# A hand-written order of 942 steps, laid anew: step order, engines, PSUM banks and output transfers of a fused attention and gMLP kernel

## The chip, the cores and the metric

The kernel runs on one core of a Trainium2 chip. The metric is device time in microseconds (us) of one execution; the times shown are the median, lowest and highest of several. A core has five engines that run their own instruction streams and meet at semaphores: TensorE (PE, with its weight loads shown apart as PEld), VectorE (DVE), ScalarE (ACT), GpSimd (POOL) and SyncE (SP), which here issues most DMA transfers.

## The reference

Input x is 2048 x 448 in bf16, with H = 16 heads of Dh = 28, and Fh = 896 channels in each half of the gMLP.

```python
mod = silu(c) @ w_mod                       # six rows: sa, ca, ga, sb, cb, gb
h = layernorm(x) * (1 + ca) + sa
q, k, v = heads(h @ wqkv)
phi(t) = concat(softmax(t @ w_phi), softmax(-(t @ w_phi)))       # for each head
kv = phi(k)^T @ v ;  z = sum over s of phi(k)
o = (phi(q) @ kv) / (phi(q) . z + 1e-6)
x = x + ga * (o @ wo)
h = layernorm(x) * (1 + cb) + sb
y = gelu(h @ w_in) ;  z1, z2 = y[:, :896], layernorm(y[:, 896:])
g = w_sp @ z2 + b_sp                        # w_sp is 2048 x 2048: mixes positions
out = x + gb * ((z1 * g) @ w_out)
```

## The kernel before, in words

**An order written out by hand.** The whole fast path is one string, ORDER (from line 482). Each word is a step: a name, its arguments after a colon, the engine after a slash (V is DVE, S is ACT, G is POOL, Y is the DMA queue of SP) and, after an @, the PSUM bank that a product goes to. A loop at the end (lines 1282 to 1294) takes the words one by one and calls the function of that name, with scheduling by hand: each engine executes its own words in the order in which they stand. There is no planner. A word's place therefore sets what it is queued behind on its engine; what it waits for on other engines follows from the tiles and banks that it reads and overwrites. PSUM has eight banks: @0 to @7 name one, @A0, @A1, @A2 and @C the pairs 0-1, 2-3, 4-5 and 6-7. A product that goes to a bank waits until the reader of that bank's former content is done.

Positions are worked in 16 tiles of 128 (index i), or in 8 pairs (index p). The stages, in order, with the step names that the prediction uses:

- *K stage.* l1s, l1e, l1r, l1a: statistics and application of the first layer norm. T1 (line 890): DMA transpose of tiles to hT, on SP. kM (908) is k times its weights, kE and kF (911) the two exponentials on ACT, kS (922, DVE), kR (926, DVE) and kP (929, DVE or POOL) the softmax. vM (916) and vC (919) make v. kA (939) accumulates phi(k)^T v of all tiles in PSUM. csB and ccB (801) make the shift and scale columns of the second norm, esB and ecB (807) read them, bc (855, 857) spreads them; gr (967) and ge (970) make the gate rows ga and gb. wos and wts (973) multiply wo and w_out by them.
- *Attention's output.* KV (945, DVE) masks the accumulated product into the right-hand side of nM. qM (956), qE and qF (961) make phi(q). For each tile nM (984, PE), nX (988, ACT), nC (991, DVE); for each pair nS (995) and nV (1000) on DVE; then for each tile nT (1003, DVE, reads the banks of nM) and nA (1010, DVE or POOL), which writes half a pair of f_oo. T2 (1013) transposes a pair on SP. wN and wM (1025, 1029, PE) multiply it by wo; wR (1034 ACT, 1036 DVE) evicts to x and sums, wQ (1041 ACT, 1043 DVE) sums squares.
- *Second norm and gMLP in.* lA, lB, lC, lD (1049 to 1058) and l2r (1061, POOL) make mean and reciprocal deviation, l2a (1065) applies them, T3 (1069) transposes a pair on SP, hS (815 ACT, 818 DVE) applies the columns. zM (1079) is the z2 half, zG (1082, ACT) its gelu, zQ its squares, zA to zD and zW its statistics, zN (1097, DVE or POOL) the normalization. yM (1104) and yG (1107) are the z1 half. W:t,u (1113) are the 32 transposing loads of w_sp on SP; W:0 has a tile of its own, W:1 and W:3 go to the tile of phi(q) (f_Eq) and W:2 to that of w_in (f_win), so they wait until these are read out.
- *Spatial product.* w_sp @ z2 in two halves of the output positions (p = 0 and 1). Six of the seven column blocks are made by a Strassen-Winograd scheme: tT (1162) are its differences of z2 blocks, sS (1174) its sums of w_sp blocks, pM:p,f,k (1185) its seven products of eight matmuls each, for f = 0 to 2; pc (1205, ACT) copies one out of PSUM, pb (1208 and 1209, POOL) adds the bias, uA, uB, uW and cA (1212, DVE) add products up, cX (1237, DVE or POOL) multiplies by z1. gM (1121) and gG (1127) are the seventh block. guard (1240) to guard3 (1252) compute the flag by which a general path would be taken: guard2 is a product of one number into a bank, guard3 reads it there, `read` (1255) loads it at the end.
- *Output.* oM (1134) is seven matmuls for a tile of 128 positions, oE (1150, DVE) adds x, oD (1153) sends the 112 KB tile out on SP. The last tile is done in two halves, oH, oG (1143, DVE) and oF (1147, on ACT's queue).

What the diff touches in code is only the string; it is read here:

```python
for word in ORDER.split():
    word, _, slot = word.partition("@")
    word, _, en = word.partition("/")
    nm, _, arg = word.partition(":")
    ...
    STEPS[nm](*[int(v) for v in arg.split(",") if v], **kw)
```

Of the kernel before, what the change touches and what calls it, by code (L numbers as in the profile page):

```python
# [490 lines left out]
kA:1@A1 qE:1 kR:3 vM:6@6 l1e:12,16/V kS:4 vM:7@4 ld:wmgb/Y l1r:12,16 kE:6 kP:3/V kA:2@A1 kS:5 kE:7 vM:4@5 l1a:15/G kF:6 kA:3@A1 l1a:12/G vC:5 kR:4 kR:5
kM:10@1 kF:7 l1a:13/V kP:5/G kS:6 vC:7 T1:12,14 kM:9@0 vC:6 kM:8@4 kP:4/V l1a:14/G vM:8@7 kR:6 kE:8 kS:7 vM:11@6 kF:8 kP:6/G T1:14,16 vC:4 kM:11@4 kR:7 kE:9
kS:8 kA:4@A1 ld:win1/Y kP:7/G kA:5@A1 kE:10 kM:13@5 kR:8 kF:9 kF:10 kS:9 ld:wo/Y vM:9@0 kP:8/G kA:6@A1 kS:10 vC:9 kA:7@A1 vC:8 W:0,2 kM:12@1 kE:11 kR:9
kR:10 kF:11 kM:14@0 kP:9/V kE:12 W:0,1 kP:10/V kA:8@A1 kF:12 kA:9@A1 kS:11 kE:14 kM:15@1 bc:0/S kS:12 vM:10@4 W:0,5 kE:13 kF:14 vM:12@7 kR:11 kF:13 kR:12
# [4 lines left out]
nM:6@A0 wR:1/S nT:5 nA:4/G nM:7@A1 nX:6 nX:7 wR:0/S nC:6 nC:7 wN:1@C nA:5/V T2:2 wQ:0/S nS:3 nV:3 nT:6 wQ:1/S nM:9@A2 wR:3/S nT:7 nM:8@A0 nA:6/G nX:9 nX:8
wR:2/S nC:9 nC:8 wN:2@A1 nA:7/V T2:3 wQ:2/S lA:2,4/G nS:4 lA:0,2/G nV:4 lB:2,4/G lB:0,2/G nT:8 wQ:3/S qM:7@C wR:5/S lC:2,4/G lC:0,2/V bc:1/G nT:9 wR:4/S  # L500
nA:8/V lD:0,2/V lD:2,4/V nM:11@A0 nA:9/V qF:7 l2r:2,4 wQ:5/V nM:10@A1 T2:4 qM:6@A2 l2a:2/V nX:11 l2a:3/G nX:10 qE:7 nC:10 nC:11 lA:4,6/G T3:1 wQ:4/S nS:5
l2r:0,2 nV:5 wN:3@C nT:10 qE:6 l2a:0/G nT:11 l2a:1/G qF:6 lB:4,6/G T3:0 wR:6/S lC:4,6/G nM:12@A0 hS:1/V nM:13@A1 wR:7/S nA:11/V nA:10/V nX:12 zM:1@A2+C
# [839 lines left out]
```

## Time and profile before

| | us |
|---|---|
| time, median of 3 runs (lowest to highest) | 248.39 (248.27 to 248.64) |
| time of the profiled execution | 248.15 |
| its span in the profile | 246.3 |
| busy: PE | 232.2 |
| busy: DVE | 195.8 |
| busy: ACT | 109.0 |
| busy: POOL | 137.3 |

The span runs from the first to the last instruction that the profile holds; the time contains some 2 us around it. A line number such as L1003 is a line of the kernel. In the tables of windows each row is a stretch of the span, its length, the busy time of PE, PEld, DVE, ACT and POOL, the granted TensorE clock, the busy share of the DMA engines and GB/s. A row of waits reads: the engine and line that waits, the engine and line it waits for, us in total, times, longest. A row of a timeline begins with start and duration in us; x8 means that so many instructions of one line stand together in it. In rows of the chain of waits the same two numbers stand ahead. An f_oo<-f_t is a tile written from a tile read.

### The profile page before, as it was taken

The numbers are of one execution on the slowest core, as the hardware profiler recorded it, in microseconds if no ns is written. First come the engines' busy times: TensorE is split into PE (matmuls) and PEld (weight loads), VectorE is DVE, ScalarE is ACT, GpSimd is POOL, SyncE is SP. The second block draws the span as 40 slices with busy tenths as digits, with TensorE's granted clock in tenths as the row PEclk, the third lists the DMA queues.
The fourth block names the chain that finished last, engine by engine and source line by source line (L and its number), as shares of the span: only waits on it lengthen the run. The fifth ranks groups of instructions, "written<-read, shape, count | busy, mean of one in ns | idle before, by whom it ended". The sixth has DMA issues, their size and how long they took to land.

```text
span 246.3 us, 4824 instructions
## 1 busy us (share of the span) xinstructions
PE 232.2 (94%) x1831; PEld 126.6 (51%) x1840; DVE 195.8 (79%) x383; ACT 109.0 (44%) x228; POOL 137.3 (56%) x173
## 2 busy tenths in 40 slices
...
GB/s 173 260 286 129 79 215 187 279 206 251 92 102 76 125 167 109 60 42 163 220 178 115 24 3 1 0 54 116 149 188 44 3 73 39 0 3 1 1 68 94
DMA packets 68130, 26.94 MB, mean 109 GB/s; under 512 B 56385, under 2 KB 67970, under 8 KB 68098
## 3 DMA queue, kind: packets, MB, share of 16 engines
...
## 4 chain that ended last, share of the span: by engine, by line
PE 72%; DVE 13%; DMA 6%; issue 3%; ACT 1%; POOL 1%; SPq 1%; DVEq 0%; POOLq 0%; ACTq 0%
PE f_psum L1185 26%; PE f_psum L1134 8%; PE f_psum L1104 8%; PE f_psum L1079 6%; PE f_psum L1121 6%; PE f_psum L908 4%; PE f_psum L916 4%; DMA f_zone<-in_w_mod_dram 3%; DVE f_t L1003 3%; PE f_psum L956 3%; PE f_psum L939 2%; PE f_psum L1029 2%; DMA f_oo<-f_oo 1%; DMA f_hT<-f_xpad 1%; PE f_psum L831 1%
## 5 line engine op out<-in xcount | busy, mean ns | idle before, releaser
L1185 PEld LDWEIGHTS <-f_zone 128*128 128x128 bf16 x192 | 18.7, 98 | 22.6 <-issue 0.4
L1185 PE MATMUL f_psum<-f_wsp,f_zone 128*128 128x512 bf16 x116 | 27.2, 379 | 0.2
L1185 PE MATMUL f_psum<-f_hT,f_Eq 128*128 128x512 bf16 x95 | 22.3, 379 | 0.1
L1079 PE MATMUL f_psum<-f_win,f_hT 64*128 64x448 bf16 x224 | 22.0, 349 | 0.4 <-DVE f_hT L818 0.4
L1104 PE MATMUL f_psum<-f_hT,f_win 64*128 64x256 bf16 (+1 forms) x294 | 22.1, 305 | 0.1
L1134 PE MATMUL f_psum<-f_wout,f_zone 128*128 128x448 bf16 x105 | 20.7, 352 | 0.0
L1237 POOL TENSOR_TENSOR f_zone<-f_win,f_zone 128x512 bf16<-128x512 f32 x9 | 11.7, 1309 | 15.0 <-DVE f_win L1212 15.0
L1205 ACT COPY f_win<-f_psum 128x512 f32<-128x512 f32 x2 | 1.2, 587 | 42.0 <-POOL f_zone L1237 37.4
L961 ACT ACTIVATE f_Eq<-f_psum 112x1024 bf16<-112x1024 f32 x16 | 16.0, 1026 | 5.8 <-PE f_psum L956 5.8
L911 ACT ACTIVATE f_zone<-f_psum 128x448 bf16<-128x448 f32 x32 | 16.3, 560 | 4.3 <-DVE f_zone L929 2.2
L1104 PEld LDWEIGHTS <-f_win 64*128 64x128 bf16 x294 | 14.4, 94 | 7.3 <-DVE f_hT L818 0.2
L1003 DVE TENSOR_TENSOR f_t<-f_psum,f_w 128x896 bf16<-128x896 f32 x16 | 16.8, 1086 | 0.6
L922 DVE TENSOR_REDUCE f_ksum<-f_zone 128x32 f32<-128x896 bf16 x16 | 16.8, 1067 | 0.5 <-ACT f_zone L911 0.5
L929 POOL TENSOR_TENSOR f_zone<-f_zone 128x896 bf16<-128x896 bf16 x8 | 13.8, 1741 | 5.8 <-DVE f_zone L926 5.5
L1079 PEld LDWEIGHTS <-f_hT 64*128 64x128 bf16 x224 | 11.0, 94 | 10.1 <-DVE f_hT L818 0.5
L1082 ACT ACTIVATE f_zone<-f_psum 128x896 bf16<-128x896 f32 x16 | 14.6, 914 | 3.0 <-PE f_psum L1079 3.0
L1107 ACT ACTIVATE f_zone<-f_psum 128x512 bf16<-128x512 f32 (+1 forms) x21 | 14.3, 739 | 3.0 <-PE f_psum L1104 2.8
L1185 PEld LDWEIGHTS <-f_Eq 128*128 128x128 bf16 x96 | 9.4, 98 | 11.3
L956 PE MATMUL f_psum<-f_hT,f_zone 113*128 113x512 bf16 (+1 forms) x64 | 15.0, 379 | 0.0
L1134 PEld LDWEIGHTS <-f_zone 128*128 128x128 bf16 x105 | 10.2, 98 | 9.3
L908 PE MATMUL f_psum<-f_zone,f_hT 113*128 113x448 bf16 (+1 forms) x64 | 14.0, 352 | 0.2 <-ACT f_zone L911 0.2
L916 PE MATMUL f_psum<-f_zone,f_hT 113*128 113x448 bf16 (+1 forms) x64 | 14.0, 352 | 0.0
...
## 6 DMA issues: line engine op xcount, KB each, us to landing
...
f_wout<-in_B_w_out_dram SPq DMA_DIRECT2D x1, 784.0 KB, 5.4
...
```

Of the source, the lines that this page charges most:

```text
L908: nc.tensor.matmul(t[:, 0, 0:D], lhsT=hT[0:KR[m], i, m, :], rhs=Wk[0:KR[m], m, :], start=(m == 0), stop=(m == KC - 1))
L911: nc.scalar.activation(out=Er[i % NR][:, s, :], in_=ps["k" + str(i)][:, 0, 0:D], func=ACT.Exp, scale=1.0 - 2.0 * s)
L916: nc.tensor.matmul(t[:, 0, 0:D], lhsT=hT[0:KR[m], i, m, :], rhs=wv[0:KR[m], m, :], start=(m == 0), stop=(m == KC - 1))
L922: nc.vector.tensor_reduce(out=ksum[:, i], in_=Er[i % NR][:].rearrange("p s (c f h) -> p (s c) h f", c=4, h=HP), axis=AX.X, op=ALU.add)
L956: nc.tensor.matmul(t[:, u, :], lhsT=Wq[0:KR[m], m, cc * CB:cc * CB + P], rhs=hT[0:KR[m], 4 * st:4 * st + 4, m, :], start=(m == 0), stop=(m ...
L961: nc.scalar.activation(out=Eq[st // 2][0:CB, 2 * c2:2 * c2 + 2, s, (st % 2) * 512:(st % 2 + 1) * 512], in_=ps["q" + str(n)][0:CB, :, :], f ...
L1003: nc.vector.tensor_tensor(out=tr[i % 2][:], in0=numv(i)[:, :, :, 0:DH], in1=wr[i // 2 % 2][:, i % 2].unsqueeze(3).to_broadcast([P, 2, H, D ...
L1079: nc.tensor.matmul(t[u][:, hf, 0:D], lhsT=hP[r, p, blk(j, u), :], rhs=win2[r, j, hf * D:(hf + 1) * D], start=(j == 0), stop=(j == KB - 1))
L1104: nc.tensor.matmul(t[:, u, 0:k * P], lhsT=win1[r, j, fc * P:(fc + 1) * P], rhs=hP[r, p:p + k, blk(j, u), :], start=(j == 0), stop=(j == KB ...
L1121: nc.tensor.matmul(g[:, 0, 0:b - a], lhsT=later["z2n"][:, s_, fc * P:(fc + 1) * P], rhs=wspT[t][:, s_, a:b], start=(s_ == 0), stop=(s_ == ...
L1134: nc.tensor.matmul(ps["o" + str(t)][:, 0, 0:D], lhsT=later["z1T"][:, fc, t * P:(t + 1) * P], rhs=wout_s[:, fc, :], start=(fc == 0), stop=( ...
L1185: nc.tensor.matmul(t[:, 0, :], lhsT=b[:, j, f * P:(f + 1) * P], rhs=a[:, j, :], start=(PSTART[k] and j == 0), stop=(j == NH - 1), skip_gro ...
```

## The change

The same 942 steps stand in another order. 84 of them go to another engine, and 140 products get other banks. The functions are untouched. What each stretch does:

- ccB moves from the middle of the K stage to behind the first two nM; ecB and csB move with it. The K stage's accumulator kv goes from @A1 to @A0.
- Around the attention's output, banks and the order of nM, qM and wN are rearranged; W transposes take other places on SP's queue, among them those ahead of T2:6.
- guard2 goes from bank 6 to bank 0, and pM:0,2,5 follows it in that bank, behind guard3, which stands behind pb:0,2 and uB:0,2.
- At the end, each oE follows its product more closely, oD:4 moves behind oD:8, and the oD of the last products stand one by one between the steps. Before, nine output transfers stand at the end.

Steps that change engine (V is DVE, G POOL, S ACT), by kind:

| step | to another engine |
|---|---|
| cX | 7 G to V, 4 V to G |
| nA | 5 G to V, 4 V to G |
| zN | 4 G to V, 4 V to G |
| wQ, zQ | wQ 10, 11, 13, 14, 15 and zQ 8 from S to V; wQ 8, 12 and zQ 3, 5, 10 from V to S |
| kP | 1 G to V, 3 V to G |
| wos, wts, l2a, tT, bc, l and z steps | the rest |

Lines of the diff (the rest is of the same kind):

```diff
-qM:1@A2 kF:2 T1:6,8 vC:2 l1s:10 m6 ge:0 T1:4,6 l1s:11 qM:0@A1 qF:1 kR:0 kS:3 l1e:8,12/G kE:2 l1r:8,12 kP:0/V ccB@7 qF:0 l1a:9/G kR:1 l1s:12 kM:5@6 qE:0
-l1a:10/G l1s:13 kM:4@1 l1a:11/G ecB vM:5@0 kS:2 kP:1/G T1:10,12 kF:4 kE:4 kM:7@7 kR:2 l1s:15 ld:wsb/Y kA:0@A1 l1a:8/G kF:5 kM:6@1 l1s:14 kE:5 kP:2/G T1:8,10
...
-kP:13/V kP:14/G qM:2@A2 kS:15 vC:14 kR:15 kP:15/V wos:0,1/G kA:13@A1 qE:2 kA:14@A1 kA:15@A1 qF:2 qM:3@A0 wos:3,4/G KV:0 KV:1 wos:1,2/G wos:2,3/V qF:3
-nM:0@A1 wos:4,5/V nM:1@A2 wos:5,6/V qM:5@C nX:0 nX:1 nC:0 qE:3 nC:1 nS:0 nV:0 nT:0 csB@0 qE:5 nT:1 gr:1@1 nA:0/G qF:5 nM:2@A1 wos:6,7/V nM:3@A2 ge:1 nA:1/V
...
-lA:6,8/G nX:13 wQ:7/S nC:12 T2:5 nC:13 lD:4,6/G l2r:4,6 nS:6 wQ:6/S nV:6 lB:6,8/G nT:12 W:0,0 gt lC:6,8/G l2a:5/G nT:13 l2a:4/G wM:4@A0 W:0,7 zG:2 lD:6,8/V
-l2r:6,8 wM:5@A1 hS:0/V zG:3 T3:2 wR:8/V nA:13/G wR:9/V yM:0,2,6@A2 W:1,1 nA:12/V lA:8,10/G l2a:7/V zM:0@A0+C l2a:6/G yG:0,2,6 wR:11/V zQ:2/S T2:6 wR:10/V
...
-pM:0,2,5@1 guard3 pc:0,2 sS:0,2,0/V pc:0,1 wts:0/G pM:0,1,2@3 tT:2,6,8/V pM:0,2,2@0 wts:3/V pM:0,0,2@7 pb:0,0 tT:3,2,4/V cA:0,1,11 gM:1,6@6 tT:3,6,8/V
-pb:0,1 tT:4,6,8/G gM:0,6@3 sS:0,3,0/V tT:4,2,4/G sS:0,3,1/V wts:1/G pM:0,1,6@4 gG:0,6 pM:0,1,7@5 gG:1,6 pb:0,2 pM:0,0,6@3 cA:0,0,11 cX:0,0,11/V pM:0,1,5@6
...
-cX:1,0,12/G gM:3,6@5 gG:2,6 cX:1,0,21/V cX:1,2,21/V oM:10,0,7@4 gG:3,6 oM:9,0,7@6 gG:4,6 oM:12,0,7@5 oH:15,1@7 read oM:11,0,7@2 oM:13,0,7@3 oE:11 oE:9
-oG:15,1 oM:14,0,7@0 oE:13 oF:15,1/S oE:10 oD:13/Y oM:8,0,7@1 oE:12 oD:10/Y oE:14 oD:12/Y oD:14/Y oH:15,0@4 oE:8 oD:11/Y oD:9/Y oG:15,0 oD:8/Y oF:15,0/S hint
+l1a:5/G qM:1@A2 kF:2 l1s:11 vC:2 T1:4,6 m6 kR:0 ge:0 l1s:12 l1e:8,12/G l1r:8,12 qM:0@A1 kP:0/V qF:1 kS:1 l1a:9/G kE:2 qE:1 l1a:10/G kS:3 kA:0@A0 kM:4@7
+l1a:11/G qE:0 kR:1 vM:7@6 kS:2 T1:10,12 kP:1/G qF:0 vM:4@4 kR:2 l1s:13 ld:wsb/Y kM:5@5 kP:2/G kR:3 kM:6@2 l1s:14 kE:5 kF:5 kA:1@A0 l1s:15 kF:4 vM:6@3
...
+vC:13 kR:15 kP:15/V kA:13@A0 wos:4,5/G qF:2 kA:14@A0 kA:15@A0 qE:2 qM:3@A1 KV:1 wos:3,4/G KV:0 wos:0,1/V qE:3 nM:0@A0 wos:6,7/V nM:1@A2 wos:2,3/V wos:5,6/V
+ccB@6 nX:0 nX:1 nC:0 qF:3 nC:1 nS:0 ecB nV:0 nM:3@A1 bc:0/G nT:1 nM:2@C nX:2 nX:3 nT:0 qM:5@A2 nA:1/G nC:2 nC:3 nA:0/V T2:0 nS:1 qM:4@A0 wos:1,2/V qF:5 nV:1
...
+ge:1 nC:12 nC:13 wQ:7/S zM:1@A0+A1 nS:6 lA:6,8/G nV:6 l2a:4/G gt nT:13 l2a:5/G nT:12 lB:6,8/G T3:2 wM:4@A2 zG:3 T2:5 hS:0/V wQ:6/S nA:12/V zM:0@C+A1 wR:8/V
+W:0,5 zG:2 lC:6,8/G lD:6,8/V wR:9/V wQ:8/S lA:8,10/G hS:2/V l2r:6,8 nA:13/V wM:5@A0 zG:1 wQ:9/V T2:6 lB:8,10/G l2a:7/G l2a:6/V zG:0 nM:15@A2 wR:11/V
...
+hS:3/S lA:10,12/V zA:2,4/G zM:2@A0+A2 l2a:9/G wR:13/V lB:10,12/V wR:12/V zA:0,2/G nT:14 nA:15/V zM:3@A1+C l2a:8/V zG:4 nA:14/V wQ:13/V T2:7 wQ:12/S wQ:10/V
...
+zW:12,14 yM:4,4,5@A2 ld:wout/Y tT:1,0,2/V yG:4,4,1 W:2,6 guard zA:10,12/G zB:10,12/G zN:12/G zQ:15/S yM:4,4,6@C W:2,4 zA:14,16/V zN:8/G zC:10,12/V yG:4,4,2
+guard2@0 pM:0,1,1@1 tT:1,6,8/V W:2,2 zD:10,12/G zQ:14/S sS:0,2,1/V zW:10,12 W:2,0 yG:4,4,6 zN:9/V pM:0,2,1@2 tT:1,4,6/V zB:14,16/G zN:11/V zN:10/V
...
+tT:2,6,8/V tT:2,4,6/V tT:4,6,8/G tT:2,2,4/V pM:0,0,2@3 pM:0,2,2@2 cA:0,1,11 wts:6/V pb:0,0 tT:3,0,2/V pM:0,0,6@7 pM:0,2,6@1 uA:0,0 pb:0,1 tT:3,6,8/V
+gM:1,6@4 tT:3,2,4/V pb:0,2 uB:0,2 pM:0,1,6@5 tT:3,4,6/V tT:4,2,4/V guard3 uA:0,2 pM:0,2,5@0 sS:0,3,0/V wts:3/V uB:0,0 gM:0,6@1 tT:4,0,2/V sS:0,3,1/V
...
+cX:1,1,12/G gM:3,6@3 cX:1,2,22/G gG:2,6 cX:1,2,21/G oM:8,0,7@2 gG:3,6 oM:9,0,7@4 cX:1,1,21/V oM:14,0,7@3 gG:4,6 oE:8 oH:15,0@5 oD:8/Y oH:15,1@2 oD:4/Y
+oG:15,0 oF:15,0/S oM:10,0,7@1 oG:15,1 oF:15,1/S oM:13,0,7@0 oE:10 oE:14 oD:10/Y oE:9 read oM:11,0,7@2 oD:14/Y oE:13 oD:9/Y oD:13/Y oM:12,0,7@1 oE:11 oD:11/Y
+oE:12 oD:12/Y hint
```

More of the change, by code (lines that the diff above doesn't have):

```diff
@@ L491 @@
[L491 to L494, printed above, removed]
@@ L499 @@
[L499 to L502, printed above, removed]
@@ L515 @@
-zN:8/V zC:12,14/V zD:12,14/V yM:4,4,2@A1 tT:2,0,2/V zQ:14/S zC:10,12/G zN:7/V zW:12,14 sS:0,1,1/V yG:4,4,3 yM:4,4,5@A2 wts:4/G tT:1,6,8/V yG:4,4,1 zN:13/G
-yM:4,4,6@A0 yG:4,4,2 wts:5/V zQ:15/S zD:10,12/G guard2@6 sS:0,1,0/V pM:0,0,1@7 W:2,5 zW:10,12 yG:4,4,6 tT:3,0,2/V W:2,7 yG:4,4,5 pM:0,0,5@2 zB:14,16/G
-zN:10/V zC:14,16/G zN:12/V zD:14,16/G pc:0,0 W:2,6 tT:3,4,6/V zW:14,16 sS:0,2,1/V pM:0,1,1@3 zN:15/G zN:11/V pM:0,2,1@0 zN:14/G tT:2,4,6/V tT:2,2,4/G
-pM:0,2,5@1 guard3 pc:0,2 sS:0,2,0/V pc:0,1 wts:0/G pM:0,1,2@3 tT:2,6,8/V pM:0,2,2@0 wts:3/V pM:0,0,2@7 pb:0,0 tT:3,2,4/V cA:0,1,11 gM:1,6@6 tT:3,6,8/V
@@ new lines @@
+ccB@6 nX:0 nX:1 nC:0 qF:3 nC:1 nS:0 ecB nV:0 nM:3@A1 bc:0/G nT:1 nM:2@C nX:2 nX:3 nT:0 qM:5@A2 nA:1/G nC:2 nC:3 nA:0/V T2:0 nS:1 qM:4@A0 wos:1,2/V qF:5 nV:1
+nT:2 W:0,6 qE:5 nT:3 nM:4@C nA:2/G nM:5@A2 nX:4 nC:4 nA:3/V wN:0@A1 nX:5 qE:4 nC:5 T2:1 nS:2 qF:4 nV:2 nT:5 nM:7@A0 wR:1/S nT:4 nA:5/G nM:6@A2 nX:7 nX:6
+wR:0/S nC:7 nC:6 wN:1@C nA:4/V T2:2 wQ:1/S lA:0,2/G nS:3 lB:0,2/G nV:3 nT:7 wQ:0/S nM:9@A1 wR:3/S lC:0,2/G nT:6 csB@0 nA:7/G wR:2/S nA:6/V nM:8@A2 nX:9
+lA:2,4/G T2:3 wN:2@C nC:9 lD:0,2/G nX:8 esB wQ:2/S nC:8 l2r:0,2 nS:4 wQ:3/S lB:2,4/G nV:4 W:0,4 l2a:0/G nT:9 qM:7@A0 lC:2,4/G wR:5/S lD:2,4/G nT:8 l2a:1/G
@@ new lines @@
+nM:14@A1 T3:3 yM:0,2,5@C wR:10/V nX:14 nX:15 nC:14 nC:15 yM:0,2,6@A0 W:0,7 yG:0,2,5 nS:7 nV:7 wM:6@C lC:8,10/V yG:0,2,6 nT:15 lD:8,10/G W:1,0 l2r:8,10
+hS:3/S lA:10,12/V zA:2,4/G zM:2@A0+A2 l2a:9/G wR:13/V lB:10,12/V wR:12/V zA:0,2/G nT:14 nA:15/V zM:3@A1+C l2a:8/V zG:4 nA:14/V wQ:13/V T2:7 wQ:12/S wQ:10/V
+zG:5 lA:12,14/V W:0,0 zB:0,2/V lB:12,14/V wQ:11/V yM:0,2,2@A0 zG:6 lC:12,14/V zQ:1/V yM:2,2,1@A2 T3:4 yG:0,2,2 yM:2,2,0@A1 zG:7 lD:12,14/V lC:10,12/V zQ:0/V
+l2r:12,14 W:0,3 yM:2,2,3@A0 yG:2,2,1 wM:7@C yG:2,2,3 lD:10,12/G l2a:12/V zQ:6/S l2r:10,12 yM:2,2,6@A2 wR:15/V zB:2,4/G l2a:10/G yG:2,2,0 yM:2,2,4@A0
```

48 lines of the change are left out of this document (25 added, 23 removed).

## The prediction

> **What bounds the kernel now.** I read the page's first part, then the table of windows by stage, then the chain of waits, and last the timelines of the queues at the places where PE stands still.
>
> ```profile
> span 246.3 us, 4824 instructions
> ...
> PE 232.2 (94%) x1831; PEld 126.6 (51%) x1840; DVE 195.8 (79%) x383; ACT 109.0 (44%) x228; POOL 137.3 (56%) x173
> ```
> ```profile
> 13.00:55.00 42.00, 41.78 (x343) 24.64 (x342) 39.51 (x83) 33.24 (x64) 31.78 (x35) 1.00 0.86 195
> 55.00:97.00 42.00, 38.30 (x417) 22.08 (x417) 39.52 (x103) 32.44 (x82) 19.49 (x37) 1.00 0.65 132
> 97.00:131.00 34.00, 34.00 (x422) 20.18 (x416) 29.41 (x68) 30.25 (x61) 26.86 (x40) 1.00 0.73 128
> 131.00:176.00 45.00, 44.58 (x206) 20.22 (x208) 38.76 (x49) 3.91 (x7) 36.04 (x28) 1.00 0.30 50
> 176.00:239.40 63.40, 63.19 (x327) 31.41 (x329) 40.77 (x60) 1.66 (x3) 16.62 (x13) 1.00 0.22 49
> 239.40:246.30 6.90, 0.03 (x1) 0.00 (x0) 0.41 (x2) 0.00 (x0) 0.00 (x0) 0.76 0.29 86
> ```
> Each row is a stretch, its length, then the busy time of PE, weight load, DVE, ACT and POOL, the granted clock and what the DMA moved. Length less PE busy is 0.22, 3.70, 0, 0.42, 0.21 and 6.87 us. The order removes no work from PE, so these gaps are all that a better order can win, and two carry nearly all of it: 3.70 us in 55 to 97 us (the attention's output, nM to zM:3) and 6.87 us after the last product. DVE is busy for 39.52 of 42 us in the first of these. The row of waits there says on whom PE waits:
> ```profile
> PEld L1029 <- DMA f_oo<-f_oo: 1.7, 3, 0.8
> PE f_psum L984 <- DVE f_t L1003: 1.3, 2, 0.8
> ```
> ```profile
> L1003 DVE TENSOR_TENSOR f_t<-f_psum,f_w 128x896 bf16<-128x896 f32 x16 | 16.8, 1086 | 0.6
> ```
> nM (L984) waits for banks that nT (L1003) reads on DVE, 1.09 us for each tile, and wM (L1029) waits for the transposed tile that follows from it. So PE is the bound up to KV, DVE and its transposes from KV to wM:6, PE again from there, and the transfers at the end.
>
> **The change part by part.** I laid out the words of the new order engine by engine, each with its duration in the rows, and compared with the place of the same step before. The sum of durations moves 6.0 us more onto DVE (an estimate, from the means of the rows on each engine) and 7.9 us off POOL. Matmul work is the same.
>
> (a) *K stage.* kM:4 now follows kA:0, where ccB stood in between:
> ```profile
> 22.79 1.26 SPq L890 DMA_TRANSPOSE f_hT<-f_xpad  x1
> ```
> ```profile
> f_hT<-f_xpad SPq DMA_TRANSPOSE x14, 3.1
> ```
> ```profile
> 25.12 0.78 PE f_psum L801 x32
> ```
> The transpose that kM:4 reads lands at 22.79 + 3.1 = 25.9 us; without the 0.78 us of ccB, kM:4 would want it at about 25.4. That is a new wait of 0.5 us. Some waits on kP and on banks go; all that they can give is the 0.22 us idle of the first row, and I take +0.2 with ends −0.2 and +0.9 (the transpose at its landing and nothing won back, plus as much again for its neighbour T1:8,10).
>
> (b) *KV to wM:6.* ccB is filled in behind KV, so KV, the start of DVE's chain, comes 0.78 − 0.2 = 0.6 us earlier. lC:0,2, lD:0,2, lD:2,4 and l2a:2 leave DVE's early part. On the queue of SP, T2:6 stood behind three W's (0,0, 0,7 and 1,1) and now behind one:
> ```profile
> 83.04 2.65 SPq L1113 DMA_TRANSPOSE f_wsp<-in_B_w_sp_dram  x2
> 85.74 2.18 SPq L1069 DMA_TRANSPOSE f_hT<-f_xpad  x1
> 87.96 1.32 SPq L1113 DMA_TRANSPOSE f_Eq<-in_B_w_sp_dram  x1
> ```
> ```profile
> 87.19 0.39 DVE L1010 TENSOR_TENSOR f_oo<-f_t 128x448 bf16<-128x448 bf16 x1
> ```
> ```profile
> 89.44 3.38 DMA f_oo<-f_oo
> ...
> 92.87 1.50 PE f_psum L1029 x14
> ```
> The sum nA:12 was done at 87.58, its transpose T2:6 was issued at 89.44 and landed at 92.82, and wM:6 began at 92.87. Without the W of 1.32 us it goes out up to 1.8 us sooner. Against it stand new waits for banks: nM:3 now has A1, which qF:3 must leave first, between 0 and the 1.03 us of one such exponential:
> ```profile
> L961 ACT ACTIVATE f_Eq<-f_psum 112x1024 bf16<-112x1024 f32 x16 | 16.0, 1026 | 5.8 <-PE f_psum L956 5.8
> ```
> qM:5 behind nT:1 is between 0 and 1.09 (the row of nT), and zM:1 behind ge:1 and hS:1 is of the same size; they fall where PE has work in hand or DVE is behind, so I let them take part of the gain and no more. The walk ends with wM:6 2.35 us earlier and the first product pM 1.85 us earlier than before. With the 0.2 lost in (a), this part alone is −2.05. The walk has no waits of 0.1 us and less, so I take −1.7; the ends are +2.5 (rival E) and −2.6 (of the 3.7 us, what does not belong to the 1.09 us bank wait).
>
> (c) *First half of the spatial product.*
> ```profile
> 131.35 1.90 PE L1185 MATMUL f_psum<-f_wsp,f_zone 128*128 128x512 bf16 x7
> ```
> ```profile
> 164.48 10.74 PE f_psum L1185 x49
> ```
> The first pM stood at 131.35, and a matmul of this stage takes 10.74/49 = 0.219 us. In the new order pM:0,2,5 comes behind ten pM and gM:1,6, 96 matmuls, so it is wanted 21.0 us after the first. It goes to bank 0, where guard2 has put its flag; guard3 reads that on DVE, and now stands behind uB:0,2, which needs pb:0,2 from POOL. POOL does tT:4,6,8, pb:0,0, pb:0,1 and the first half of pb:0,2 before, and starts once tT:2,6,8 is done on DVE. For that:
> ```profile
> 134.62 0.56 DVE L1162 TENSOR_TENSOR f_zone<-f_zone 128x768 bf16<-128x768 bf16 x1
> ...
> 140.06 1.99 DVE L1162 TENSOR_TENSOR f_Eq<-f_zone,f_Eq 128x768 bf16<-128x768 bf16 x1 [0.92 <-POOL f_zone L1097]
> ...
> 143.11 1.50 DVE L1162 TENSOR_TENSOR f_zone<-f_zone 128x768 bf16<-128x768 bf16 x1
> ```
> ```profile
> 160.90 0.68 DVE L1212 TENSOR_TENSOR f_Eq<-f_psum,f_Eq 128x512 f32<-128x512 f32 x1
> 161.49 0.38 DVE L973 TENSOR_TENSOR f_wout<-f_wout,f_g_rep 128x448 bf16<-128x448 bf16 x1
> ```
> ```profile
> 139.99 1.64 POOL L1162 TENSOR_TENSOR f_Eq<-f_zone,f_Eq 128x768 bf16<-128x768 bf16 x1
> ...
> 142.90 1.30 POOL L1208 TENSOR_TENSOR f_t<-f_Eq,f_bsp 128x512 f32<-128x512 f32 x1
> 144.28 1.35 POOL L1209 TENSOR_TENSOR f_Eq<-f_Eq,f_bsp 128x512 f32<-128x512 f32 x1
> ...
> 147.13 2.21 POOL L1209 TENSOR_TENSOR f_Eq<-f_Eq,f_bsp 128x512 f32<-128x512 f32 x1
> 149.30 4.22 POOL L1162 TENSOR_TENSOR f_oo<-f_zone,f_Eq 128x768 bf16<-128x768 bf16 x2
> ```
> ```profile
> 192.78 1.15 POOL L1208 TENSOR_TENSOR f_CBT<-f_Eq,f_bsp 128x512 f32<-128x512 f32 x1 [11.61 <-ACT f_Eq L1205]
> ```
> Before, tT:2,6,8 ended 142.05 − 131.35 = 10.7 us after the first pM; in the walk it ends at 8.9 if each step takes its shorter row. From there, the short rows: 1.64 + 2 x 1.15 + 2 x 1.15 + 1.15 on POOL, then 0.68 (uB:0,2) and twice 0.56 (tT:3,4,6 and tT:4,2,4) on DVE: 18.1 us, early by 2.9. The long rows: 10.7 + 4.22/2 + (1.30 + 1.35) + (1.30 + 2.21) + 1.30 + 0.68 + 2 x 1.50 = 24.0, late by 3.0. The middle is just in time; but an early flag wins nothing and a late one costs its whole lateness, so over the range from 2.9 early to 3.0 late the mean cost is about 3.0/4, and I take +0.8, with ends 0 and 3.0.
>
> The row of 1.50 against that of 0.56 shows what DVE loses beside POOL. [...]
>
> DVE also meets wts:1 before tT:2,6,8, and this needs w_out, whose load stands on SP behind W:2,1, which overwrites weights that zM:7 reads:
> ```profile
> f_wout<-in_B_w_out_dram SPq DMA_DIRECT2D x1, 784.0 KB, 5.4
> ```
> zM:7 ends three yM ahead of the first pM. Even if the two went out only with the first pM, w_out would be there after 1.3 + 5.4 = 6.7 us, and wts:1 (0.38), sS:0,2,0 (about 1.2, by its neighbours) and tT:2,6,8 (0.56) would end at 8.8, not past the 8.9 above: no cost of its own.
>
> (d) *Second half and the products with w_out.* PE's idle time before is 0.21 in the last but one row. I found no step there that is wanted before it is made; the tightest (uA:1,0, oE:4, cX:1,1,21) have 0.3 to 0.9 us in hand. Zero, with ends 0 and +0.9. The change of engine of cX, nA, wts and the small l and z steps beside them is covered by PE's queue of products; without it each costs about its own row.
>
> (e) *The end.* Before, SP sent seven of the transfers one behind the other, for 5.28 us from 236.84 on.
> ```profile
> 236.84 5.28 SPq L1153 DMA_DIRECT2D out_dram<-f_xpad  x7
> ```
> ```profile
> L1150 DVE TENSOR_TENSOR f_xpad<-f_psum,f_x 128x448 bf16<-128x448 f32 x15 | 8.7, 616 | 4.6 <-PE f_psum L1134 4.6
> ```
> ```profile
> 244.00:246.30 2.30, 0.00 (x0) 0.00 (x0) 0.00 (x0) 0.00 (x0) 0.00 (x0) 0.50 0.00 0
> ```
> ```profile
> DMA to landing us min/median/max: 1.7/1.8/3.9
> ```
> Nothing moves in the last 2.3 us of the span. In the new order each oE follows its product and each oD its oE; the last, oM:12, oE:12, oD:12, has one transfer in front of it. So after the last matmul: 0.62 + 1.8 + 2.3 = 4.7 us where 6.9 were, −2.2. With the longest landing, 3.9, it is 6.8 and −0.1. Ten transfers of 112 KB go out over some nine microseconds, so the median is the nearer; `read` stands on SP between them, and I take −1.8.
>
> **Sum** against the profiled execution, which took 248.15 us (span 246.3 and 1.85 around it): +0.2 − 1.7 + 0.8 + 0 − 1.8 = −2.5, so 245.65. The median of the runs, 248.39, is 0.24 above it: 245.9.
>
> **Rivals.**
> B: part (b) gives nothing, because DVE remains the bound and the waits for banks eat what the earlier KV and T2:6 win: 245.9 + 1.7 = 247.6. For it: 39.5 of 42 us busy on DVE; against it: T2:6 did stand ready for 1.9 us.
> C: the end is still bunched, the last transfer lands in 3.9 us: 245.9 + 1.7 = 247.6. For it: `read` in front of five of the transfers; against it: the order of the oE.
> D: the flag comes at its latest, 3.0 in place of 0.8: 248.1, no change that can be told. For it: rows of 2.21 and 1.50; against it: DVE has less to do in this stretch that reads two tiles from SBUF.
> E, slower: DVE's chain in (b) becomes longer.
> ```profile
> L1036 DVE SCALAR_TENSOR_TENSOR f_x<-f_psum,f_x 128x448 bf16<-128x448 f32 x6 | 3.6, 617 | 0.0
> ```
> Between KV and nT:14 DVE gets wR:12 and wR:13 (2 x 0.62), bc:1 (about 0.6, by the same row), two wos more and ecB, and loses one l2a, one wQ, and lC and lD against lA, lB, lC: about +1.5 by the rows. If it has no gaps to put them in, the stretch grows by 1.5, and by 1.0 more if nM:3's wait for qF:3 idles it: 245.9 + 1.7 + 2.5 = 250.1. It is slower than before once (b) is above +1.3. For it: 0.6 us is all the idle time in front of sixteen nT; against it: several of these stood later, past the last nT that wM:6 needs.
>
> **How the numbers follow.** Forecast 0.46, B 0.12, C 0.12, D 0.12, E 0.18. About 0.2%, 0.5 us (247.9 to 248.9), is what a measurement of this kernel can tell from no change. So faster 0.70, same 0.12, slower 0.18. The forecast's own range is 243.8 (the tail at −2.2, no wait in (c), (b) at −2.6) to 247.4 ((c) at 2.3). The range reaches up to B, C and D and to the bound of "same": 243.8 to 248.8; E is outside.
>
> **What the profile after would show.** (a) PE at kM:4 waiting for the transpose by some 0.5 us, and KV earlier. (b) PE's idle time between nM and zM:3 near 2 us, T2:6 issued within a microsecond of nA:12, wM:6 near 90.5; if PE's wait on L1003 has grown, E or B. (c) the first pM near 129.5, and a gap on PE at pM:0,2,5 of at most 3 us, released by DVE at L1252; none if POOL kept its short rows. (d) PE without a gap from there to the last oM. (e) at most 5 us from the last matmul to the end, SP's last transfer alone. The prediction is wrong if PE stands still at a step I priced at nothing: above all at the four pM that read the last zN of POOL, of which fewer products stand ahead now, or behind wts:1 on DVE.

## The result, and the profile after

The changed kernel takes 245.28 us, median of 4 runs (244.7 to 246.06), where the kernel before takes 248.40 (248.27 to 248.64): a ratio of 0.9875, 95% interval 0.9845 to 0.9906. In a later comparison, the last of the experiments, the ratio was 0.9912 (0.9878 to 0.9947). The forecast was 245.9. The profiled execution took 244.99 us; its span is 243.1 us against 246.3, which is 3.2 us less.

The page of the changed kernel, and its windows (length, then busy PE, PEld, DVE, ACT, POOL, then granted clock, DMA share and GB/s). Lines of the kernel are one higher than before, since the string has one line more:

```profile
span 243.1 us, 4826 instructions
...
PE 232.3 (96%) x1840; PEld 129.7 (53%) x1840; DVE 195.1 (80%) x396; ACT 107.7 (44%) x225; POOL 123.8 (51%) x163
```
```profile
0.00:13.00 13.00, 11.32 (x137) 8.71 (x138) 8.11 (x26) 7.73 (x15) 6.45 (x23) 1.00 0.94 247
13.00:55.00 42.00, 41.63 (x351) 24.84 (x350) 38.02 (x81) 33.60 (x67) 34.92 (x39) 1.00 0.88 214
55.00:97.00 42.00, 39.32 (x424) 22.54 (x425) 39.60 (x106) 30.85 (x80) 21.54 (x39) 1.00 0.60 106
97.00:131.00 34.00, 34.00 (x408) 22.92 (x405) 28.29 (x69) 31.06 (x60) 23.20 (x33) 1.00 0.67 130
131.00:176.00 45.00, 44.99 (x222) 20.87 (x220) 40.16 (x61) 3.32 (x6) 22.89 (x19) 1.00 0.38 71
176.00:236.00 60.00, 60.00 (x304) 29.43 (x302) 39.87 (x59) 1.17 (x2) 14.73 (x12) 1.00 0.14 34
236.00:243.10 7.10, 1.08 (x6) 0.36 (x4) 1.04 (x2) 0.00 (x0) 0.00 (x0) 0.84 0.29 88
```

PE is busy for the same time as before (232.3 and 232.2), so only its idle time has changed. In 55 to 97 us it is 2.68 where it was 3.70, and behind 131 us it is gone but for the end. Before, the first stretch looked like this:

```profile
0.00:13.00 13.00, 10.31 (x130) 8.05 (x131) 7.46 (x24) 7.51 (x14) 6.56 (x23) 1.00 0.95 221
```

The DMA engines moved 221 GB/s there and now 247, and PE has done 1.0 us more of work by 13 us. To split the time I follow four landmarks on PE: kM:0, the first nM, the first pM and the end of the last product. The timelines of PE, before and then after, have the first two:

```profile
14.19 1.69 PE L908 MATMUL f_psum<-f_zone,f_hT 113*128 113x448 bf16 x8
54.92 1.00 PE L984 MATMUL f_psum<-f_KVbd,f_Eq 112*128 112x120 bf16 x16
```
```profile
13.34 1.69 PE L909 MATMUL f_psum<-f_zone,f_hT 113*128 113x448 bf16 x8
52.98 1.00 PE L985 MATMUL f_psum<-f_KVbd,f_Eq 112*128 112x120 bf16 x16
53.81 0.94 PE L802 MATMUL f_psum<-f_zone 112*128 112x1 bf16 x32
55.17 1.00 PE L985 MATMUL f_psum<-f_KVbd,f_Eq 112*128 112x120 bf16 x16 [0.42 <-ACT f_Eq L962]
56.68 1.68 PE L957 MATMUL f_psum<-f_hT,f_zone 113*128 113x512 bf16 x7 [0.50 <-DVE f_t L1004]
129.16 5.35 PE L1186 MATMUL f_psum<-f_wsp,f_zone 128*128 128x512 bf16 x24
```

| piece, us | before | after | moved |
|---|---|---|---|
| start to kM:0 | 14.19 | 13.34 | −0.85 |
| kM:0 to nM:0 (K stage) | 40.73 | 39.63 | −1.10 |
| nM:0 to first pM | 76.43 | 76.18 | −0.25 |
| first pM to end of last product | 108.08 | 107.92 | −0.16 |
| from there to the span's end | 6.92 | 6.03 | −0.89 |

The chain of waits after shows that PE does not stand still from 84 us to the last product; five of its pieces from there on, and the last three, are

```profile
84.01 2.82 PE f_psum L1080 x28
86.84 1.32 PE f_psum L1030 x14
88.16 0.95 PE f_psum L985 x16
89.11 1.64 PE f_psum L1105 x28
90.74 1.43 PE f_psum L1030 x14
...
231.78 5.31 PE f_psum L1135 x28
237.09 0.03 issue
237.12 0.62 DVE f_xpad L1151
```

### The profile page after: what moved, and what is told of

It reads as the page before. It is cut to its first block, busy times and chain, and to the rows that moved or that the text cites. A ratio compares the mean times of both kernels' runs of the same rounds, so it can differ in the third digit from the quotient of the medians.

```text
span 243.1 us, 4826 instructions
## 1 busy us (share of the span) xinstructions
PE 232.3 (96%) x1840; PEld 129.7 (53%) x1840; DVE 195.1 (80%) x396; ACT 107.7 (44%) x225; POOL 123.8 (51%) x163
## 4 chain that ended last, share of the span: by engine, by line
PE 72%; DVE 13%; POOL 6%; issue 4%; DMA 3%; ACT 0%; DVEq 0%; POOLq 0%
PE f_psum L1186 30%; PE f_psum L1105 9%; PE f_psum L1135 8%; PE f_psum L1080 8%; PE f_psum L1122 6%; DVE f_t L1004 5%; PE f_psum L917 3%; POOL f_xpad L886 2%; PE f_psum L940 2%; PE f_psum L909 2%; DMA f_hT<-f_xpad 2%; PE f_psum L1030 2%; DVE f_zone L875 2%; PE f_psum L957 1%; POOL f_zone L883 1%
## 5 line engine op out<-in xcount | busy, mean ns | idle before, releaser
L1105 PEld LDWEIGHTS <-f_win 64*128 64x128 bf16 x294 | 16.1, 94 | 5.4
L930 POOL TENSOR_TENSOR f_zone<-f_zone 128x896 bf16<-128x896 bf16 x10 | 17.3, 1745 | 2.0 <-DVE f_zone L927 1.3
L1080 PEld LDWEIGHTS <-f_hT 64*128 64x128 bf16 x224 | 12.2, 94 | 10.2 <-DVE f_hT L819 1.9
L1108 ACT ACTIVATE f_zone<-f_psum 128x512 bf16<-128x512 f32 (+1 forms) x21 | 15.2, 739 | 2.1 <-PE f_psum L1105 2.0
L917 PE MATMUL f_psum<-f_zone,f_hT 113*128 113x448 bf16 (+1 forms) x64 | 14.5, 352 | 0.0
L1213 DVE TENSOR_TENSOR f_win<-f_psum,f_win 128x512 f32<-128x512 f32 x16 | 10.8, 682 | 4.4 <-PE f_psum L1186 4.3
```

Of the source, the lines that this page charges most:

```text
L917: nc.tensor.matmul(t[:, 0, 0:D], lhsT=hT[0:KR[m], i, m, :], rhs=wv[0:KR[m], m, :], start=(m == 0), stop=(m == KC - 1))
L930: eng.tensor_tensor(out=pr[i % NR][:, 0:2 * D].rearrange("p (a f h) -> p a f h", a=8, h=HP), in0=Er[i % NR][:].rearrange("p s (c f h) -> p ...
L1080: nc.tensor.matmul(t[u][:, hf, 0:D], lhsT=hP[r, p, blk(j, u), :], rhs=win2[r, j, hf * D:(hf + 1) * D], start=(j == 0), stop=(j == KB - 1))
L1105: nc.tensor.matmul(t[:, u, 0:k * P], lhsT=win1[r, j, fc * P:(fc + 1) * P], rhs=hP[r, p:p + k, blk(j, u), :], start=(j == 0), stop=(j == KB ...
L1108: nc.scalar.activation(out=stage_b()["z1T"][:, fc, p * 256:(p + k) * 256].rearrange("p (j u t) -> p u j t", j=k, u=2), in_=ps["y%d_%d" % ( ...
```

## The experiments

The whole time spreads widely from execution to execution: in the first comparison below twenty of twenty-two executions of the kernel before took from 245.7 to 249.0 us, the other two still longer. So each experiment is read by its pieces; these are worked out from the starts of the same instructions in each profile. Six of the kernels below (before again, the three made from the kernel before, three W and place of oD words) ran only once, under the profiler; their single times prove nothing. The pieces differ between executions too: the K stage takes 40.56 to 40.73 us in the four profiles that have its old order and 39.36 to 40.22 in the eight that have its new one (means 40.66 and 39.82).

| kernel | to kM:0 | K stage | nM:0 to first pM | to last product | end |
|---|---|---|---|---|---|
| before | 14.19 | 40.73 | 76.43 | 108.08 | 6.92 |
| before again | 13.75 | 40.66 | 76.69 | 108.08 | 7.17 |
| before, ccB moved | 14.10 | 40.93 | 77.33 | 108.15 | 7.20 |
| before, T2:6 first | 13.95 | 40.56 | 76.45 | 108.08 | 7.83 |
| before, order of the oE | 13.84 | 40.69 | 76.77 | 108.22 | 5.13 |
| changed | 13.34 | 39.63 | 76.18 | 107.92 | 6.03 |
| changed again | 14.52 | 39.36 | 77.82 | 107.93 | 5.96 |
| changed, ccB back | 13.14 | 40.45 | 76.09 | 107.92 | 5.28 |
| changed, place of oD words | 13.17 | 39.52 | 76.21 | 107.92 | 5.34 |
| changed, oE:9, oE:14 early | 13.40 | 40.07 | 76.21 | 107.92 | 5.89 |
| changed, read early too | 13.23 | 39.76 | 76.21 | 107.93 | 6.23 |
| changed, three W | 13.56 | 40.05 | 79.27 | 107.92 | 5.89 |
| changed, hint early | 13.46 | 39.92 | 77.83 | 107.92 | 5.44 |
| changed, qM:5 ahead | 13.54 | 40.22 | 76.34 | 107.92 | 5.77 |

**ccB back in the K stage.** The theory is that PE bounds the K stage, so that ccB taken out of it is won in full; the rival, that the earlier KV is lost behind it.

```diff
-kA:0@A0 kM:4@7 ... qE:0 kR:1 vM:7@6 ... ccB@6 nX:0 ... nS:0 ecB nV:0
+kA:0@A0 ccB@6 kM:4@7 ... qE:0 kR:1 ecB vM:7@6 ... nX:0 ... nS:0 nV:0
```

> The changed order with one thing undone: ccB stands between kA:0 and kM:4 again, and ecB behind kR:1. Compared with the changed kernel (245.28 us). Theory (PE is the bound up to KV, so what is taken out of it there arrives in full, and the stretch after KV has idle time on PE to hide ccB): KV and nM:0 come 0.8 to 1.0 us later, and so does the end: 246.1 to 246.3. Rival (the earlier KV is lost again while DVE is the bound, and the gain came from elsewhere): no change, 245.3, with wM:6 at the same place.

The K stage took 40.45 us, longer than in any of the eight profiles with ccB out of it and by 0.6 us longer than their mean; the rest to the first pM took 76.09, the same as in the changed kernel within 0.1 us. So 0.6 us are lost ahead of nM:0 (0.8 against the first profile alone) and nothing is won behind it. Against the kernel before the ratio was 0.9936 (0.9904 to 0.9969), where two other variants of the changed order in the same comparison had 0.989 (0.984 to 0.994 and 0.986 to 0.992). The intervals overlap; profile and times both point to the theory.

**One part alone: ccB moved in the kernel before.**

```diff
-kP:0/V ccB@7 qF:0 ... l1a:11/G ecB vM:5@0 ... kM:15@1 bc:0/S kS:12 ... nT:0 csB@0 qE:5 nT:1 gr:1@1 nA:0/G qF:5
+kP:0/V qF:0 ... l1a:11/G vM:5@0 ... kM:15@1 kS:12 ... nT:0 ccB@1 ecB csB@0 qE:5 nT:1 gr:1@1 nA:0/G bc:0/G qF:5
```

> The kernel before with one part of the change alone: ccB, ecB and bc:0 leave the K stage and stand behind nT:0, ahead of csB. Time from kM:0 to nM:0 was 40.73 us before and 39.64 in the changed kernel. Theory (ccB is 0.78 us of a stretch in which PE is the bound): 39.9 to 40.2, and the first pM earlier by 0.4 to 0.8 against kM:0. Rival (kM:4 and kM:5 then wait for their transpose for as long as ccB took): 40.5 to 40.8.

The rival holds, and more: 40.93 us. The waits of PE in 14 to 56 us say why; in the kernel before the row on the DMA is not there.

```profile
PE f_psum L908 <- DMA f_hT<-f_xpad: 1.1, 2, 0.6
```

PE then waits twice for its transposed tiles, 1.1 us together, and behind nM:0 0.6 to 0.9 us more are lost, about the length of ccB. This is the wait that the prediction priced at 0.5 us. In the changed order it does not come at kM:4, because l1a and T1:4,6 stand earlier too: T1:4,6 goes out at 21.23 us and lands at 24.26, where it was 22.79 and 25.86; kM:4 begins at 24.53. At the neighbour, T1:8,10, it does come, in five of the nine profiles of the changed order and its variants, for 0.2 to 0.7 us; in the variant with oE:9 and oE:14 early, at kM:8:

```profile
34.14 0.93 PE L909 MATMUL f_psum<-f_zone,f_hT 113*128 113x448 bf16 x4 [0.54 <-DMA f_hT<-f_xpad]
```

This is most of the spread of the K stage. The gain of the K stage is that of two moves together: ccB moved alone makes it 0.3 us longer (40.93), the rest of the new order alone 0.2 shorter (40.45), both 0.8 shorter (39.82, mean of eight).

**Three W in front of T2:6 again.**

```diff
-wQ:9/V T2:6 ... yM:0,2,6@A0 W:0,7 yG:0,2,5 ... lD:8,10/G W:1,0 l2r:8,10
+wQ:9/V W:0,7 W:1,0 T2:6 ... yM:0,2,6@A0 yG:0,2,5 ... lD:8,10/G l2r:8,10
```

> The changed order with one thing undone: W:0,7 and W:1,0 stand ahead of T2:6 on SP again, so that three W's do. In the changed kernel SP reaches T2:6 at 85.9 us, waits for nA:12 until 86.92, and the transpose lands at 89.94; wM:6 begins at 90.74 with no wait. Theory: two more W's of 1.3 us put T2:6 out at about 88.5, it lands at about 91.4, PE waits some 0.7 us in front of wM:6, and everything behind is later by that. Rival: the landing is not what wM:6 turns on, no wait, same times from wM:6 to the last product.

The waits of PE in 55 to 97 us have a row that the changed kernel has not:

```profile
PE f_psum L1030 <- DMA f_oo<-f_oo: 1.4, 1, 1.4
```

So the place of T2:6 is worth 1.4 us in the new order, in this one profile. In the changed kernel SP's timeline shows it out at once (nA:12 ends at 86.92):

```profile
84.49 1.31 SPq L1114 DMA_TRANSPOSE f_wsp<-in_B_w_sp_dram  x1
86.98 1.22 SPq L1014 DMA_TRANSPOSE f_oo<-f_oo  x1
```

The time from nM:0 to the first pM grew by 3.1 us, though. The other 1.65 us have nothing to do with the edit: see the clock, below.

**The same alone in the kernel before: W:1,1 behind T2:6.**

```diff
-yM:0,2,6@A2 W:1,1 nA:12/V ... T3:3 hS:2/V ... W:1,3 nX:15
+yM:0,2,6@A2 nA:12/V ... T3:3 hS:2/V ... W:1,1 W:1,3 nX:15
```

> The kernel before with W:1,1 moved from in front of T2:6 to behind T3:3. T2:6 was issued at 89.44 us and landed at 92.82, wM:6 began at 92.87. Theory: T2:6 goes out 1.3 us sooner, wM:6 and all behind it come 0.5 to 0.8 us sooner against nM:0 (PE has yM:0,2,5 until then). Rival: PE finds no work sooner and waits elsewhere for DVE: no change of the first pM against nM:0 (76.43 us).

From nM:0 to the first pM it was 76.45 us, where the kernel before has 76.43: the rival. PE's wait of 0.5 us for the transpose is gone, and no first pM is earlier by it.

**The end.** Five kernels. First, only the places of the words in the text:

```diff
-oE:8 oH:15,0@5 oD:8/Y oH:15,1@2 oD:4/Y ... oE:11 oD:11/Y oE:12 oD:12/Y hint
+oE:8 oH:15,0@5 oH:15,1@2 ... oE:11 oF:15,0/S oF:15,1/S oD:8/Y oD:4/Y oD:10/Y oD:14/Y oD:9/Y oD:13/Y oD:11/Y oE:12 oD:12/Y hint
```

> The changed order, with the words of the last output transfers put behind the last oE in the text and in the same order on SP's queue as before the edit, and the two oF behind them on ACT's own queue. SP's own order among its transfers is not altered, so each can still go when its oE is done: theory, nothing moves by more than 0.3 us (245.3); if the place in the text alone makes the transfers wait, all nine go after 237.7 and the end comes 2 to 3 us later.

Nothing waited: oD:8 still went out 0.03 us behind its oE. The end was 5.34 us in place of 6.03 and the time 243.96 us, a difference that the next rows show to be that of executions. So "nine at the end" in the text is no reason for nine at once; before, it was the order of the oE on DVE, where oE:11 stood in front of all others and waited for its product.

```diff
-oE:11 oE:9 oG:15,1 ... oE:13 oF:15,1/S oE:10 oD:13/Y ... oE:12 oD:10/Y oE:14 oD:12/Y oD:14/Y oH:15,0@4 oE:8 oD:11/Y oD:9/Y oG:15,0 oD:8/Y oF:15,0/S
+oE:10 oE:9 oE:12 oD:10/Y oD:9/Y oD:12/Y ... oG:15,1 oF:15,1/S oE:11 oD:11/Y ... oE:13 oD:13/Y oE:14 oD:14/Y oH:15,0@4 oE:8 oD:8/Y oG:15,0 oF:15,0/S
```

> The kernel before with another part alone: each of the last oE on DVE stands in the order in which its product ends, each oD behind its oE, with PE's order as it was. Before, the span ended 6.92 us after the last product. If what counts is how many transfers are under way at the end: about 4.8 us. If the last transfer is held by something at the end of PE's program, as the 16 KB packets of the instruction queue suggest in the profiles of the changed kernel (one of 1.0 to 1.7 us starts 1.1 us after PE's last product, and one of the sixteen shares of the last transfer lands 2 us behind the other fifteen): 5.2 to 6.2 us.

That order alone, in the kernel before, made the end 5.13 us, against 6.92 to 7.83 in four profiles without it; that lies between the two expectations (4.8, and 5.2 to 6.2). Its one time was 246.45 us beside 248.53. The gain of this part is shown by itself, in one profile. Then the changed order with two more of its transfers taken out of the last four microseconds, and with `read` out of SP's way:

```diff
-oE:8 oH:15,0@5 oD:8/Y ... oE:10 oE:14 oD:10/Y oE:9 read ... oD:14/Y oE:13 oD:9/Y oD:13/Y
+oE:8 oD:8/Y oE:9 oD:9/Y oH:15,0@5 oE:14 oD:14/Y ... oE:10 oD:10/Y read ... oE:13 oD:13/Y
```

> The changed order with oE:9 and oE:14 put ahead of the two oG on DVE, and oD:9 and oD:14 behind them on SP: these two tiles are sent about 4 to 5 us sooner, so four in place of six transfers fall into the last 4 us. Theory (the last transfers land 3.6 to 3.9 us after their issue because too many of them are under way at once): the last one lands in 1.8 to 2.4 us, the span ends 1.2 to 1.8 us earlier, 243.5 to 244.1. Rival (the late landing belongs to the last transfer whatever stands before it): no change, 245.3.

> As e3, and the load of the flag (read) is put ahead of gM:2,6, some 15 us sooner on every engine, so that SP has 0.8 us more between the last transfers. Theory: the transfers ahead of the last start up to 0.8 us sooner; as the last waits for its oE, the end gains 0 to 0.4 us on e3: 243.2 to 244.1. Rival: the same as e3 within 0.2 us, because SP was not what the transfers waited for.

In the second the word `read` stands ahead of gM:2,6. Ends of 5.89 and 6.23 us, times of 244.76 (ratio 0.9889, 0.9843 to 0.9936) and 245.14 (0.9892, 0.9859 to 0.9924): the rivals hold. With four transfers in place of six the last one still landed 3.44 and 3.79 us after its issue, while oD:11, just ahead of it, took 1.72 and 1.89. The packets in the trace of the second (start, duration, bytes; the last transfer was issued at 237.81):

```
fifteen of its sixteen shares      last bytes by 239.2
238.73   1.700 us   16384 B   instruction queue
239.27   0.542 us    8192 B   instruction queue
240.42 to 241.06    8 packets of 896 B, the sixteenth share
```

The sixteenth share begins where a 16 KB packet of the instruction queue ends; that the two share a DMA engine is concluded from these times, since the trace does not name a packet's engine. All fourteen profiles have such a packet behind PE's last product; it starts 1.1 to 3.2 us after it, 0.7 to 1.4 us behind the end of PE's branch past the general path, and takes 0.9 to 1.7 us. In six of the fourteen the last share or two stand apart from the rest, as here, and begin within 0.02 us of the packet's end; in seven more the bytes run past that end without a gap. In the fourteenth, the one with the order of the oE, the last share begins at the end of an 8 KB instruction packet, ahead of the 16 KB one, and its landing, 2.61 us, is the shortest of all (the span ends 2.50 us behind it, where the others end 1.75 us behind theirs). In the others it took 2.8 to 3.8. That PE's branch brings the packet was the author's estimate, from its place behind the end of that branch in all fourteen. Whether the hint could move it was tried:

```diff
-oE:12 oD:12/Y hint
+hint gM:3,6@3 ... oE:12 oD:12/Y
```

> The changed order with its last word, hint (it tells the sequencers where the branch past the general path goes), moved from the end to ahead of gM:3,6, some 15 us sooner. In five profiles of the changed order and its variants the last transfer lands 2.8 to 3.8 us after its issue, and in the one looked at packet by packet fifteen of its sixteen shares land in 1.4 us and one, behind a 16 KB packet of the instruction queue on the same DMA engine, 2 us later; PE's branch starts some 3 us ahead of PE's last product and ends behind it. Theory (that packet belongs to the branch, and the hint fetches it sooner): no 16 KB packet after the last product, last landing 1.7 to 2.2 us after its issue, the span ends 4.3 to 4.8 us behind the last product (5.3 to 6.0 in the changed order's profiles), 243.8 to 244.5 us. Rival (the fetch belongs to where PE's program goes on, whatever the hint): as the changed kernel.

The packet still came, 1.6 us behind the last product; the last landing took 3.00 us; the time was 244.52 us, ratio 0.9874 (0.9832 to 0.9915), no different from the changed kernel. The rival's forecast holds; what brings the packet is not shown.

**The start.** The kernel before, for a second profile, and at the end the changed one:

> The kernel before, as it is, for a second profile beside one of the changed order on the same chip. kM:0 began at 14.19 us in its first profile, at 13.84 to 14.10 in three kernels made from it, and at 13.14 to 13.56 in six of the changed order, though the order of the loads is the same. Theory (the first loads arrive at another rate from one execution to the next): between 13.2 and 14.2, within 0.3 us of the run beside it. Rival (the changed order's start is faster): 13.8 to 14.2, and the run beside it below 13.6.

> The changed kernel as it is, for the spread of its times on one chip beside the one with qM:5 moved, and for one more profile of its start, its clock and its end. Theory: two groups of times some 1.65 us apart, 244.0 to 244.9 and 245.7 to 246.5; kM:0 at 13.1 to 13.6, the first pM 115.8 us behind it where the clock stays up and 117.5 where it falls; the last landing 2.8 to 3.8 us behind its issue. Rival: one group with one width, whatever the clock does in the profile.

kM:0 began at 13.75 us in the one (13.46 in the run beside it) and at 14.52 in the other, which is later than in any profile of the kernel before. The late start of that one profile is not that of its loads. PE's products ahead of it are slower; the changed kernel's first profile, then the second:

```profile
5.53 2.00 PE L852 MATMUL f_psum<-f_ident,f_Eq 112*112 112x112 bf16 x32
```
```profile
5.83 3.24 PE L852 MATMUL f_psum<-f_ident,f_Eq 112*112 112x112 bf16 x32
```

and the first record of a granted clock of 1.00 stands at 9.87 us there, at 4.1 to 7.2 in the other thirteen. The load of w_mod that goes out at 3.2 us, for which PE waits in the kernel before, landed at 9.73 to 10.52 us in all nine profiles of the changed order and its variants, the late one among them, and at 10.73 to 11.06 in all five of the old order. So the earlier start, 0.6 us in the means without the late profile (13.36 and 13.97), goes with the changed order, as the rival says, though its bounds were not met (13.75 was below its 13.8). Yet each engine has the same words in the same order up to kM:0: what brings the loads in sooner is not shown.

The times of the changed kernel were 244.5 to 247.4 us in six runs, one group and not two: for the times the rival holds. The profile fits the theory but for its start: 117.2 us from kM:0 to the first pM with the clock down, and a last landing of 3.52.

**qM:5 ahead.** Three of the profiles of the changed order have a stretch with the clock down (see the last section). Here qM:5 fills the stretch ahead of it:

```diff
-ccB@6 nX:0 ... nM:3@A1 bc:0/G nT:1 nM:2@C nX:2 nX:3 nT:0 qM:5@A2 nA:1/G
+ccB@6 qM:5@A1 nX:0 ... bc:0/G nT:1 nM:2@C nM:3@A2 nX:2 nX:3 nT:0 nA:1/G
```

> The changed order with qM:5 put directly behind ccB, in bank pair A1 in place of A2; nM:3 goes to A2, and from nM:5 on the pairs A1 and A2 are exchanged throughout. In two of seven profiles of the changed order and its variants the granted clock fell to 0.50 for about 3 us from 57 us on, and PE lost 1.65 us there; ahead of it stand four small nM, the 32 one-column matmuls of ccB and two waits, 3.7 us in which PE does little. Here the 1.74 us of qM:5 stand in the middle of these. Theory (the little work there brings the clock down in some executions): the clock stays at 1.00 there, executions 1.65 us longer than the rest go away, at a cost of 0.2 to 0.5 us in all, because nM:2 and nM:3 come later; median 244.5 to 245.2 and the slowest below 245.8. Rival (the clock falls for another reason, or not more often than elsewhere): the times spread as those of the changed kernel beside it, 0.2 to 0.5 us higher.

The clock stayed up in its one profile, and nM:0 to the first pM took 0.16 us more than in the changed kernel's first. Its times were 244.1 to 246.55, median 245.27, beside 245.52 (244.51 to 247.38) of the changed kernel. None of its seven executions has a low mean clock, where about one in five of the changed order has (last section); that speaks for the theory, but seven are too few to tell. No version was found that is clearly faster than the changed kernel.

## Why the prediction was right, point by point

The total was right (245.9, measured 245.28), in part by luck. Term by term the forecast was −1.5 for (a) and (b), +0.8, 0 and −1.8; the first pair of profiles has −1.35, −0.16 for (c) and (d) together, −0.89, and −0.85 at the start. What (c) did not cost and what (e) did not give cancel, and the start was not foreseen.

- *(a) K stage.* Mis-sized. Predicted +0.2 and, with ccB out, nM:0 0.6 us earlier; it was 1.10 earlier than kM:0 explains. Over all profiles it is 0.84. The failing step is the new wait of 0.5 at kM:4: it took the transpose T1:4,6 from the old order, where it went out at 22.79, and the new order sends it 1.56 us sooner. The wait came at the neighbour T1:8,10, which the prediction had only in its upper end, and in five profiles of nine. ccB alone is 0.94 us of PE in the rows above; a wait of 0.2 us for kE went too.
- *(b) KV to wM:6.* Mis-sized. Predicted −1.7 with the earlier KV in it, measured −0.25 behind nM:0. The prediction shows no working for the 1.7 (its 0.6 and 1.8 less half of 1.03 would be 1.9), and the 0.2 of (a) is taken off a second time in the 0.6. T2:6 and wM:6 came as said (issued 0.06 us behind nA:12; wM:6 at 90.74, forecast 90.5), but wM:6 is 2.1 us early only because nM:0 is 1.9 us early. The step that failed is the 1.8 us for T2:6: it left nA:12 at its old place, and the new order of DVE ends nA:12 33.9 us behind nM:0 where it was 32.7. So T2:6 went out 0.5 us sooner against nM:0, and wM:6 began 0.2 sooner. What the stretch did give is that it took in the 0.94 us of ccB at no cost where the clock stayed up. Rival B was right on this stretch, by its reason: DVE stayed the bound, 39.60 of 42 us busy.
- *(a) and (b) together* were to bring the first pM 1.5 us forward; they brought it 1.35.
- *(c) The flag.* Taken at +0.8, it cost nothing. guard3 on DVE's timeline:

```profile
147.92 0.14 DVE L1253 TENSOR_SCALAR flag<-f_psum 1x1 int32<-1x1 f32 x1
```

  It ended 18.9 us after the first pM, near the 18.1 of the short rows; pM:0,2,5 came at 149.89 without a wait. tT:2,6,8, which I had between 8.9 and 10.7 us after the first pM, was done by 7.9, when POOL began tT:4,6,8, and the halves of pb took 1.16 to 1.47 us, none of them 2.21. From that start the short rows alone (9.2 us) give 17.1. Of the 1.8 us above that, 1.2 are in POOL's rows up to the first half of pb:0,2, which ended at 145.68, and 0.6 in DVE's behind it. What DVE lost beside POOL stands in the same trace: a tT, which reads two tiles from SBUF, took 1.50 us at 140.50, beside pb on POOL, and 0.55 at 147.45, with POOL idle, while a step that adds from PSUM took 0.68 at 139.24, beside a pb, and 0.67 at 147.99, with POOL idle. It cost no wait, and rival D did not come.
- *(d)* Right. From the first pM to the last product PE has no gap in the first profile of the changed kernel, and one of 0.2 us in seven of the other eight.
- *(e) The end.* Predicted −1.8. The first pair shows −0.89. Over the profiles that have the oE in the old order (6.92, 7.17, 7.20, 7.83, mean 7.28) and those of the changed order and its variants (nine, mean 5.76) it is −1.5. The end after the change is 0.69 us to the last issue, 3.59 to its landing and 1.75 to the end of the span; before, it was 2.03, 3.14 and 1.75. So the order of the oE won 1.34 us, of which a longer landing took 0.45 back. The step that failed is the landing: the median of 1.8 us came from seven transfers in the middle of the kernel (1.7 to 1.8), while the six at its end whose landing the trace shows took 2.9 to 3.9 before the change already; and the last bytes of the last one come behind a 16 KB packet of the instruction queue (1.62 us after the change, 1.43 before). The 2.3 us behind it were 1.75. The other step, one transfer late on SP, was right. Rival C had the right landing time (3.6 against its 3.9), for a reason other than bunching.
- What was not foreseen: 0.85 us at the start, 0.6 in the means. It hid that (e) fell short in the profiled pair.
- Rival E's chain came, its time did not. From nM:0 to the end of the last nT it is 41.55 us where it was 40.05, the +1.5 that E had worked out, with DVE busy for 39.1 in place of 37.8. But PE stands still nowhere behind 84 us: no product waited for the last nT. PE's waits on nT from 55 to 97 us fell, from 2.5 to 1.1 us.
